# A fused attention and expert kernel: the second MLP's input weights get their tiles at the upper end of SBUF during attention, and are converted in another order

## The chip, the core and the metric

One core of a Trainium2 chip. The time is device time of one execution, in microseconds (us), of the whole program; a profiled execution gives the trace. Engines: PE multiplies, DVE and ACT do elementwise work, POOL (GpSimd) too, SP starts nearly all DMAs. Each engine works through its own list of instructions in order; they wait for one another by semaphores.

## What is computed

Attention over 4 sequences of 576 positions, 8 heads of 64, as a coarse part (every 4 positions averaged, softmax over 144) plus a local part (a band of 3 to either side); its rows x (2304 x 512) go through eight experts, one for each row, and then a second MLP:

```python
attn_out = coarse(q, k, v) repeated 4 times along the sequence + local(q, k, v)
e = argmax(x @ w_gate + bias[modality]);  x = gate * (relu(x @ w1[e]) @ w2[e])
h = x @ w_in                              # 512 -> 2048
out = (max(h,0) + alpha*min(h,0)) @ w_out # 2048 -> 512
```

`w_in` and `w_out` arrive as float64. The products behind the gate are done in three passes over a high and a low half (f32r) of each operand, so each weight is converted: 64-bit words to float32, then split into two halves.

## The kernel before

The stages follow one another. **Attention** (to about 261 us): `down(b)` is a list of steps for one sequence's coarse part (stageA transposes, stageV averages v on POOL, stageB, stageT, stageE, stageP); they are laid between the 24 local tiles of 96 rows (`local1a` to `gate3`). For each tile the gate is the product `lg` on PE, then small steps on DVE (`l`, maximum, index, one-hot `oh`), then the rank product `rk`, whose rows are scattered by POOL. The coarse part of sequence b+1 is made beside the tiles of sequence b, so it is done when sequence 3 begins (n = 18 of 24). Rows of the fullest expert start early (`Early`, products `ph` and `py`, five groups): their products stand in PE's list between those of the tiles. The last count `cnt` then leads into `plan` (some 45 small DVE steps), which fills the table `r_tab` from which SP takes where rows are loaded. At `tc.If(rare>0)` each engine loads a flag and branches; the block behind it isn't run here.

**Slots** (seven, to about 450 us): each takes 256 rows of one expert. `load_x(s+2)` asks for rows L, POOL scales them, DVE transposes (T) and splits them; PE makes `h` (96 products of 256 columns) and `y` (96); ACT and DVE make the halves `hh` and `hl` of h and those of the weights (`w1h`/`w1l`, `w2h`/`w2l`). **Second MLP** (`moe2`): five blocks of rows, `oh` then `oy`; in block 0 the 32 pieces of w_out are converted as they are needed (`W2out`).

A piece of w_in is 128 rows x 256 columns; there are 32. `W2in_load(i)` asks for one (256 KB, on SP, into a ring of three stage buffers `raw64`, shared with w_out), and `from64` converts it: L555, L556, L557 on DVE into one of two float32 tiles, the cast `wih` on ACT, the subtraction `wil` on DVE (for w_out: `wol` on POOL). The tiles wih and wil (64 KB of each partition) are opened behind attention. Pieces 0 and 1 stand behind the first slot's row preparation, 2 to 23 in the slots (four in each, from f = 0 to 3), 24 to 31 in block 0.

```python
            if f<4 and 4*s+f<22:
                with tc.issue_after(d.ins), tc.issue_after(after[0].ins): W2in(AT0+4*s+f)
```

Pools are taken from SBUF in the order of the code, and a tile laid on memory of a closed pool waits for the last reader there. The order of each engine's list is set by a scheduler from the order and priorities of the code.

Of the kernel before, what the change touches and what calls it, by code (L numbers as in the profile page):

```python
# [16 lines left out]
def attention(ctx, tc, q, k, v, mod, wg, bias, xs, running, ps, eps, zeros, early):  # L17
# [7 lines left out]
    loading=ExitStack(); ld=loading.enter_context(tc.tile_pool(name="a_load",bufs=1))  # L25
# [43 lines left out]
    KD=cp.tile([128,4,2,GD],F32,name="kdb"); nc.gpsimd.memset(KD,0.0)  # L69
    QD=cp.tile([128,4,2,GT],F32,name="qdb"); nc.gpsimd.memset(QD,0.0)  # L70
# [17 lines left out]
    KB=[cp.tile([128,4,2,SP],F32,name=f"kb{i}") for i in range(2)]  # L88
    QT=[cp.tile([128,4,SP],F32,name=f"qt{i}") for i in range(2)]
# [100 lines left out]
    def stageB(b,pair):  # L190

        e=ed[b,pair]=wk.tile([128,2,GD],F32,tag="ed",name=f"ed{b}{pair}",bufs=4)
# [3 lines left out]
        if pair==0: ek[b]=wk.tile([128,H,GT],F32,tag="ek",name=f"ek{b}",bufs=1)  # L196
# [3 lines left out]
    def stageT(b):  # L200

        e=wk.tile([128,1,GD],F32,tag="edt",name=f"edt{b}",bufs=1)
# [5 lines left out]
        eb=wk.tile([128,H,GT],F32,tag="eb",name=f"eb{b}",bufs=1)  # L208
# [3 lines left out]
    def stageE(b,i):  # L212
        if i==0: EM[b]=wk.tile([128,H,GD],F32,tag="em",name=f"em{b}",bufs=1)
# [165 lines left out]
class Router:  # L379

    def __init__(self, tc, rp, cp):
# [24 lines left out]
        self.xr=rp.tile([1,NSP],I32,name="r_xr"); self.yl=rp.tile([1,1],I32,name="r_yl"); self.ok=c([1,NSP+1],"r_ok"); nc.vector.memset(self.ok[:,0:1],1.0)  # L406
        self.rare=rp.tile([1,1],I32,name="r_rare"); self.tab0=rp.tile([1,4],I32,name="r_tab0")
# [221 lines left out]
def moe(tc, stack, router, wts, rows, ep, fp, W2in):  # L629
# [67 lines left out]
    def slot(s):  # L697
# [13 lines left out]
        for f in range(8):  # L711
# [13 lines left out]
            if f<4 and 4*s+f<22:  # L725
                with tc.issue_after(d.ins), tc.issue_after(after[0].ins): W2in(AT0+4*s+f)
# [40 lines left out]
def moe2(tc, stack, wp, tp, fp, ep, win, first, W2out, W2in, al, ysT, ytok, out):  # L767
# [12 lines left out]
    def block(j):  # L780
# [43 lines left out]
def body(tc,q,k,v,mod,wg,bias,w1,w2,w_in,w_out,alpha,out):  # L824
    nc=tc.nc
    with ExitStack() as ctx:
# [10 lines left out]
        early=Early(tc,ep,eps,rows,wts)  # L837
        with ExitStack() as a:
# [5 lines left out]
            for n in attention(a,tc,q,k,v,mod,wg,bias,xs,running,ps,eps,lambda: rows.zeros(E*N),early):  # L844
# [8 lines left out]
                if n in EARLY:  # L853
# [6 lines left out]
        wip=ctx.enter_context(tc.tile_pool(name="w_in",bufs=1))  # L860
        wir=wip.tile([128,4,F2],F32R,name="wih"); wil=wip.tile([128,4,F2],F32R,name="wil")
        fp=ctx.enter_context(tc.tile_pool(name="first",bufs=1))
        wst=ctx.enter_context(tc.tile_pool(name="w_stage",bufs=3))
        staged={}
        def w_out_rows(f,u):
            r=staged[f,u]=wst.tile([128,256,2],I32,tag="raw64",name=f"wo{f}{u}")
            nc.sync.dma_start(r.rearrange("p d w -> p (d w)"),w_out[128*f:128*f+128,256*u:256*u+256].bitcast(I32))


        PIECES=[(c,p) for c in (3,2,1,0) for p in range(6)]+[(c,p) for p in range(6,8) for c in range(4)]  # L870
        def W2in_load(i):
# [64 lines left out]
```

## Time and profile before

| | |
|---|---|
| three runs | 852.78, 853.17 and 861.1 us, median 853.17 |
| profiled execution | 859.48 us, its span 857.7 us |
| busy in the span | PE 806.6 us (94%), DVE 536.4 (63%), ACT 361.1 (42%), POOL 193.6 (23%) |
| mean granted clock of PE | 0.972 of 2.4 GHz |
| moved by DMA | 71.73 MB, 84 GB/s on average |

PE's busy time is a bad measure of how full PE is, since products are pipelined; what it loses is read from its idle stretches and from what ended them. Times in rows count from the span's start.

### The profile page before, as it was taken

To read this page: it belongs to the slowest core of one execution; us is meant where nothing else is said; L and a number is where in the kernel's file an instruction comes from. 1 tells how busy PE (TensorE), PEld (TensorE's weight loads), DVE (VectorE), ACT (ScalarE), POOL (GpSimd) and SP (SyncE) were. 2 spreads that over 40 slices of the span, in tenths; PEclk is the share of its full clock that TensorE was granted. 3 is DMA by queue.
4 is the path that set the end of the run, shared out by engine and by line. 5 is a ranking of instruction groups with operands and counts; after the bars stand their busy time and mean duration, and the time that the engine had idled before them with its cause. 6 is when DMAs were issued, how large, how long until landed. Compare 5 with 4: busy or idle time off the path is not lost.

```text
span 857.7 us, 16919 instructions
## 1 busy us (share of the span) xinstructions
PE 806.6 (94%) x6247; PEld 694.5 (81%) x6247; DVE 536.4 (63%) x1365; ACT 361.1 (42%) x863; POOL 193.6 (23%) x390
## 2 busy tenths in 40 slices
PE   4799898989998889999999998999999999999997
PEld 3477687768898889999998867888888888888895
DVE  6866857557525789999859899563344333533361
ACT  7698686786422655666542233221111111111120
POOL 9424645337441000111002223200010001000100
PEclk9779989989999999999999999999999999999999
DMA  7745666322313432459313344200020001000100
GB/s 194 174 104 156 190 186 170 98 48 55 87 45 97 88 101 75 101 118 288 78 38 103 119 138 143 88 26 1 3 83 7 1 1 62 6 1 1 49 2 24
DMA packets 96608, 71.73 MB, mean 84 GB/s; under 512 B 40456, under 2 KB 83976, under 8 KB 96520
## 3 DMA queue, kind: packets, MB, share of 16 engines
q1 hardware_dynamic: 93544, 61.02, 27.2%
q0 software_dynamic: 2976, 9.59, 3.1%
q8 instruction: 50, 0.82, 0.4%
q14 instruction: 38, 0.31, 0.2%
HBM read 76.43 MB, written 18.90 MB: 111 GB/s over the span
## 4 chain that ended last, share of the span: by engine, by line
PE 48%; DVE 9%; DMA 5%; issue 3%; ACT 1%; SPq 1%; POOL 0%; POOLq 0%; DVEq 0%; ACTq 0%
PE oh L798 18%; PE oy L787 18%; PE h L719 6%; PE y L739 6%; DMA wo<-in_moe_w_out 2%; DVE xwo L557 1%; DMA oT<-ysT 1%; DMA L<-xs 1%; DVE xwo L556 1%; DVE w1l L548 1%; DVE xwo L555 1%; DMA wi<-in_moe_w_in 1%; DVE m L800 1%; DVE m L801 1%; DVE xwi L557 1%
## 5 line engine op out<-in xcount | busy, mean ns | idle before, releaser
L547 ACT CAST gh<-m 128x512 fp32r<-128x512 f32 (+1 forms) x80 | 44.5, 557 | 230.7 <-DVE m L801 227.7
L798 PE MATMUL oh<-oxh,wih 128*128 128x512 f32 (+1 forms) x320 | 117.6, 367 | 0.0
L798 PE MATMUL oh<-oxl,wih 128*128 128x512 f32 (+1 forms) x320 | 117.6, 367 | 0.0
L798 PE MATMUL oh<-oxh,wil 128*128 128x512 f32 (+1 forms) x320 | 117.6, 367 | 0.0
L787 PE MATMUL oy<-woh,gh 128*128 128x512 f32 x272 | 106.2, 393 | 3.3 <-ACT woh L547 3.2
L787 PE MATMUL oy<-wol,gh 128*128 128x512 f32 x272 | 107.0, 394 | 1.1 <-POOL wol L548 1.1
L800 DVE TENSOR_SCALAR m<-oh,al 128x512 f32<-128x512 f32 (+1 forms) x80 | 55.5, 694 | 83.5 <-PE oh L798 83.5
L787 PE MATMUL oy<-woh,gl 128*128 128x512 f32 x272 | 106.0, 391 | 0.0
L815 POOL DMA_INDIRECT out<-o,tt x18 | 18.0, 998 | 279.9 <-ACT o L814 244.6
L548 DVE TENSOR_TENSOR gl<-m,gh 128x512 fp32r<-128x512 f32 (+1 forms) x80 | 49.2, 615 | 36.6 <-ACT gh L547 36.4
L719 PE MATMUL h<-xh,w1h 128*128 128x256 f32 x224 | 63.6, 285 | 6.9 <-DVE hl L722 6.9
L798 PEld LDWEIGHTS oh<-oxh,wil 128*128 128x128 f32 x320 | 60.2, 188 | 10.6
L798 PEld LDWEIGHTS oh<-oxh,wih 128*128 128x128 f32 x320 | 60.1, 188 | 10.6
L798 PEld LDWEIGHTS oh<-oxl,wih 128*128 128x128 f32 x320 | 60.2, 188 | 10.0
L787 PEld LDWEIGHTS oy<-woh,gh 128*128 128x128 f32 x272 | 51.3, 189 | 15.1 <-ACT woh L547 4.9
L719 PE MATMUL h<-xh,w1l 128*128 128x256 f32 x224 | 63.2, 282 | 0.1
L719 PE MATMUL h<-xl,w1h 128*128 128x256 f32 x224 | 63.1, 282 | 0.0
L787 PEld LDWEIGHTS oy<-wol,gh 128*128 128x128 f32 x272 | 51.4, 189 | 12.5 <-POOL wol L548 2.5
L739 PE MATMUL y<-hh,w2h 128*128 128x256 f32 x224 | 60.9, 280 | 0.0
L739 PE MATMUL y<-hh,w2l 128*128 128x256 f32 x224 | 60.6, 280 | 0.1
L787 PEld LDWEIGHTS oy<-woh,gl 128*128 128x128 f32 x272 | 51.5, 189 | 10.6
L739 PE MATMUL y<-hl,w2h 128*128 128x256 f32 x224 | 58.7, 280 | 0.5 <-DVE hl L722 0.5
(305 smaller groups left out, 1821.1 us busy)
## 6 DMA issues: line engine op xcount, KB each, us to landing
wraw<-in_moe_w SPq DMA_DIRECT2D x56, 512.0 KB
wi<-in_moe_w_in SPq DMA_DIRECT2D x32, 256.0 KB
wo<-in_moe_w_out SPq DMA_DIRECT2D x32, 256.0 KB
vw<-in_v SPq DMA_DIRECT2D x88, 64.0 KB
xs<-z SPq DMA_DIRECT2D x8, 528.0 KB
ldq<-in_q SPq DMA_DIRECT2D x16, 256.0 KB
ldk<-in_k SPq DMA_DIRECT2D x16, 256.0 KB
ldv<-in_v SPq DMA_DIRECT2D x8, 512.0 KB
```

The source lines that it names most:

```text
L547: nc.scalar.copy(hi,x)
L548: return lo_engine.tensor_tensor(out=lo,in0=x,in1=hi.bitcast(F32),op=ALU.subtract)
L555: nc.vector.tensor_scalar(out=xi,in0=hw,scalar1=0x07ffffff,scalar2=3,op0=ALU.bitwise_and,op1=ALU.logical_shift_left)
L556: nc.vector.scalar_tensor_tensor(out=xi,in0=lw,scalar=29,in1=xi,op0=ALU.logical_shift_right,op1=ALU.bitwise_or)
L557: nc.vector.scalar_tensor_tensor(out=xi,in0=hw,scalar=-(1<<30),in1=xi,op0=ALU.bitwise_and,op1=ALU.bitwise_or)
L719: nc.tensor.matmul(h,lhsT=a[:,c],rhs=b[:,c],start=n==0,stop=n==11); n+=1
L739: nc.tensor.matmul(y,lhsT=a[:,f],rhs=b,start=n==0,stop=n==23); n+=1
L787: nc.tensor.matmul(y[t],lhsT=a[:,ts],rhs=b[:,f],start=f==0 and k==0,stop=f==15 and k==2)
L798: nc.tensor.matmul(h[:,:n],lhsT=a[:,c,fs],rhs=b[:,c],start=k==0,stop=k==11); k+=1
L800: nc.vector.tensor_scalar(out=m[:,:n],in0=h[:,:n],scalar1=0.0,scalar2=al[:,f:f+1],op0=ALU.min,op1=ALU.mult)
L801: nc.vector.scalar_tensor_tensor(out=g[:,:n],in0=h[:,:n],scalar=0.0,in1=m[:,:n],op0=ALU.max,op1=ALU.add)
L815: nc.gpsimd.indirect_dma_start(out=out[:],out_offset=bass.IndirectOffsetOnAxis(ap=ti[:,t:t+1],axis=0),in_=o[:],in_offset=None,bounds_check ...
```

## The change

Attention's pools for tiles that only the coarse part uses (with KB and QT of the even sequences) move to the upper end of SBUF and are closed when sequence 3's tiles begin. There the tiles of w_in and the stage ring are opened at once. Two pieces are converted behind each of the last eight tiles (`TAIL`, 16 pieces), two behind the first slot's row preparation as before, two in each of the seven slots (`SLOT`, at f = 1 and 3), and none in block 0. The pieces now go by columns first (p, then c). A one-element tile shares another's memory.

```diff
-    loading=ExitStack(); ld=loading.enter_context(tc.tile_pool(name="a_load",bufs=1))
+    loading=ExitStack(); gp,gk,ld=[loading.enter_context(tc.tile_pool(name=n,bufs=1,side="right")) for n in ("a_gone","a_down","a_load")]
...
-    KD=cp.tile([128,4,2,GD],F32,name="kdb"); nc.gpsimd.memset(KD,0.0)
+    KD=gp.tile([128,4,2,GD],F32,name="kdb"); nc.gpsimd.memset(KD,0.0)
...
-            vd[b]=wk.tile([128,H,D],F32,tag="vd",name=f"vd{b}",bufs=2)
+            vd[b]=gk.tile([128,H,D],F32,tag="vd",name=f"vd{b}",bufs=2)
...
         at(local1b,n+2); go()
+        if n==len(seq)-NT:
+            assert not fill; loading.close()
         yield n
-    loading.close()
...
-LEAD=1; WLOAD=tuple([0, 0, 1, 2, 2, 3, 3, 4]); EARLY=tuple([3, 6, 10, 14, 16]); AT0=2; LATE=28
+LEAD=1; WLOAD=tuple([0, 0, 1, 2, 2, 3, 3, 4]); EARLY=tuple([3, 6, 10, 14, 16]); AT0=2; TAIL=dict.fromkeys(range(16,24),2); SLOT=(1,3); LATE=28
...
-            if f<4 and 4*s+f<22:
-                with tc.issue_after(d.ins), tc.issue_after(after[0].ins): W2in(AT0+4*s+f)
+            if f in SLOT:
+                with tc.issue_after(d.ins), tc.issue_after(after[0].ins): W2in()
...
                 W2out(f,woh,wol)
-                if f<8: W2in(f)
...
+        win=[]; staged={}; done=set()
+        def open_w_in():
+            wip=ctx.enter_context(tc.tile_pool(name="w_in",bufs=1,side="right"))
+            win.extend((wip.tile([128,4,F2],F32R,name="wih"),wip.tile([128,4,F2],F32R,name="wil")))
+            win.append(ctx.enter_context(tc.tile_pool(name="w_stage",bufs=3,side="right")))
+            W2in_load(0)
...
+        PIECES=[(c,p) for p in range(8) for c in range(4)]
...
+        def W2in(ahead=2):
+            i=len(done)
+            if i>=len(PIECES): return
+            for j in range(i+1,i+ahead+1):
+                if ("in",j) not in staged and j not in done: W2in_load(j)
+            c,p=PIECES[i]; ps=slice(256*p,256*p+256); done.add(i)
+            from64(nc,win[2],f"wi{c}{p}",win[0][:,c,ps],win[1][:,c,ps],staged.pop(("in",i)),nc.vector)
...
+                if n==min(TAIL): open_w_in()
+                for _ in range(TAIL.get(n,0)): W2in()
             with tc.high_priority(500): router.plan(psum,running,cp)
```

What this makes of the engines' lists, at three places. (The number behind a tile's name is its buffer; lines of the changed kernel are one to three higher.)

DVE, in the tail, from the rank of one tile (`jk`, `ng`) to the gate `l` of the next; before, with the gate steps ahead of it:

```order
L287 TENSOR_TENSOR xts_4109<-pv_4100,ot_3532 128x384
L306 TENSOR_TENSOR oh_3946<-io_294,i_3943 96x8
L313 RECIPROCAL x_126<-ng_3948 96x4
L326 ISA jk_4035,ng_3948<-rk_4029,oh_3946 96x8
L326 ISA ng_3948 96x1
L581 STREAM_TRANSPOSE Te_3498<-Le_3492 128x512
L301 TENSOR_TENSOR l_4065<-lg_4052,bsel 96x8
```

The same place now:

```order
L326 ISA jk_4087,ng_3984<-rk_4081,oh_3982 96x8
L326 ISA ng_3984 96x1
L549 TENSOR_TENSOR wil<-xwi_4338,wih 128x256
L558 SCALAR_TENSOR_TENSOR xwi_4346<-wi_4264,xwi_4346 128x256
L556 TENSOR_SCALAR xwi_4412<-wi_4336 128x256
L549 TENSOR_TENSOR wil<-xwi_4346,wih 128x256
L557 SCALAR_TENSOR_TENSOR xwi_4412<-wi_4336,xwi_4412 128x256
L556 TENSOR_SCALAR xwi_4420<-wi_4344 128x256
L558 SCALAR_TENSOR_TENSOR xwi_4412<-wi_4336,xwi_4412 128x256
L557 SCALAR_TENSOR_TENSOR xwi_4420<-wi_4344,xwi_4420 128x256
L301 TENSOR_TENSOR l_4117<-lg_4104,bsel 96x8
```

Eight steps of conversions stand where one transposition stood.

PE, from the last count to the branch, before:

```order
L410 MATMUL cnt<-running_4361,r_one 1x8
L932 BRANCH_PREFETCH_HINT
L602 MATMUL py_3803<-eh_3501,wraw 128x128 x8
L602 MATMUL ph_3860<-Te_3835,wraw 128x128 x4
L602 MATMUL ph_3866<-Te_3835,wraw 128x128 x4
L602 MATMUL ph_3872<-Te_3835,wraw 128x128 x4
L602 MATMUL ph_3902<-Te_3835,wraw 128x128 x4
L602 MATMUL ph_3964<-Te_3835,wraw 128x128 x4
L602 MATMUL ph_3987<-Te_3835,wraw 128x128 x4
L602 MATMUL ph_3993<-Te_3835,wraw 128x128 x4
L602 MATMUL ph_3999<-Te_3835,wraw 128x128 x4
L602 MATMUL py_4080<-eh_3838,wraw 128x128 x8
```

Behind these comes the branch (L901). Now:

```order
L411 MATMUL cnt<-running_4493,r_one 1x8
L935 BRANCH_PREFETCH_HINT
L603 MATMUL ph_4039<-Te_3843,wraw 128x128 x4
L603 MATMUL ph_4045<-Te_3843,wraw 128x128 x4
L603 MATMUL ph_4051<-Te_3843,wraw 128x128 x4
L603 MATMUL py_4132<-eh_3846,wraw 128x128 x8
L524 TENSOR_LOAD r_rare
L903 COMPARE_AND_BRANCH
```

Of 48 early products behind the count 20 are left; 28 moved ahead of it.

SP, from the last weight load of slot 0 to the rows L of slot 2, before:

```order
L542 DMA wraw<-in_moe_w 128x8x128
L520 TENSOR_LOAD r_tab x2
L567 ISA
L567 DMA xs<-z 1024x1x132
L875 DMA wi_10263<-in_moe_w_in 128x512
L875 DMA wi_10546<-in_moe_w_in 128x512
L520 TENSOR_LOAD r_tab
L572 ISA
L572 DMA L_10340<-xs 32x8x132
```

And now:

```order
L543 DMA wraw<-in_moe_w 128x8x128
L521 TENSOR_LOAD r_tab x2
L568 ISA
L568 DMA xs<-z 1024x1x132
L852 DMA wi_10687<-in_moe_w_in 128x512
L521 TENSOR_LOAD r_tab
L573 ISA
L573 DMA L_10459<-xs 32x8x132
```

One load of w_in stands ahead of the rows where two stood.

## Rows read from the trace of the kernel before

**Rows 1.** Busy time by stretch: us, busy (x instructions), granted clock, DMA share, GB/s

```profile
core 0: us, PE busy (x) PEld busy (x) DVE busy (x) ACT busy (x) POOL busy (x), PEclk, DMA share, GB/s
200.00:220.00 20.00, 20.00 (x367) 16.71 (x362) 14.63 (x76) 12.15 (x44) 15.19 (x36) 1.00 0.28 65
220.00:240.00 20.00, 20.00 (x229) 17.52 (x228) 8.02 (x42) 7.77 (x24) 8.02 (x18) 1.00 0.29 72
...
360.00:380.00 20.00, 19.32 (x163) 18.92 (x162) 19.29 (x44) 11.92 (x26) 0.00 (x0) 1.00 0.43 124
380.00:400.00 20.00, 18.18 (x156) 17.78 (x155) 19.16 (x38) 13.17 (x29) 2.42 (x1) 1.00 0.91 225
460.00:480.00 20.00, 20.00 (x90) 16.57 (x89) 18.21 (x41) 5.70 (x12) 3.45 (x5) 1.00 0.33 104
...
520.00:540.00 20.00, 17.83 (x71) 14.06 (x70) 19.76 (x41) 6.21 (x14) 7.66 (x11) 0.91 0.38 120
```

**Rows 2.** PE's waits, whole span: us in total, times, longest us

```profile
PE h L719 <- DVE hl L722: 6.9, 6, 3.0
...
PE py L602 <- SPq L901: 3.3, 1, 3.3
PE oy L787 <- ACT woh L547: 3.2, 3, 1.7
```

**Rows 3.** Costliest groups, PE: busy, mean ns, idle before and releaser

```profile
L787 PE MATMUL oy<-wol,gh 128*128 128x512 f32 x272 | 107.0, 394 | 1.1 <-POOL wol L548 1.1
...
L739 PE MATMUL y<-hl,w2h 128*128 128x256 f32 x224 | 58.7, 280 | 0.5 <-DVE hl L722 0.5
```

**Rows 4.** Timeline of PE: start us, us, what, [idle before it and releaser]

```profile
283.16 2.05 PE L602 MATMUL py<-eh,wraw 128*128 128x128 f32 x16 [1.71 <-ACT eo L611]
...
318.15 0.53 PE L719 MATMUL h<-xh,w1h 128*128 128x256 f32 x1 [3.00 <-DVE hl L722]
...
532.54 0.50 PE L787 MATMUL oy<-woh,gh 128*128 128x512 f32 x1 [1.73 <-ACT woh L547]
```

**Rows 5.** Busy time by stretch, behind three waits of PE (columns as in Rows 1)

```profile
318.00:322.00 4.00, 3.85 (x19) 3.86 (x20) 4.00 (x9) 2.26 (x6) 0.00 (x0) 0.57 0.28 91
532.00:537.00 5.00, 4.01 (x10) 2.98 (x11) 4.89 (x10) 1.21 (x3) 2.34 (x3) 0.66 0.50 159
275.00:279.00 4.00, 3.69 (x33) 3.69 (x34) 2.13 (x6) 0.93 (x2) 0.00 (x0) 1.00 0.02 6
```

**Rows 6.** Timeline of PE from the last count to behind the branch

```profile
260.94 0.17 PE L410 MATMUL cnt<-running,r_one 96*1 96x8 bf16 x1
...
262.93 7.31 PE L602 MATMUL ph<-Te,wraw 128*128 128x128 f32 x64
270.07 1.95 PE L602 MATMUL py<-eh,wraw 128*128 128x128 f32 x16
275.31 0.94 PE L602 MATMUL py<-eh,wraw 128*128 128x128 f32 x6 [3.29 <-SPq L901]
```

**Rows 7.** Timeline of DVE in a slot, a stretch without idle

```profile
309.98 0.28 DVE L555 TENSOR_SCALAR xwi<-wi 128x256 int32<-128x256 int32 x1
310.18 0.42 DVE L722 SCALAR_TENSOR_TENSOR hl<-h,hh 128x256 fp32r<-128x256 f32 x1
...
311.31 0.42 DVE L556 SCALAR_TENSOR_TENSOR xwi<-wi,xwi 128x256 int32<-128x256 int32 x1
311.65 0.42 DVE L741 COPY yo<-y 128x256 f32<-128x256 f32 x1
```

**Rows 8.** Timeline of SP's queue, then of DVE, ahead of 318.15

```profile
300.39 4.83 SPq L875 DMA_DIRECT2D wi<-in_moe_w_in  x2
305.80 1.93 SPq L572 DMA_DIRECT2D L<-xs  x4
...
315.94 1.25 DVE L581 STREAM_TRANSPOSE T<-L 128x1024 f32<-128x1024 f32 x1 [3.21 <-POOL L L579]
```

**Rows 9.** Conversions of w_out on DVE: duration ns min/median/max, first and last start

```profile
L556 DVE SCALAR_TENSOR_TENSOR xwo<-wo,xwo x32: 408/416/966, 421.4 to 538.5; 128x256 int32<-128x256 int32 x32
L557 DVE SCALAR_TENSOR_TENSOR xwo<-wo,xwo x32: 409/420/968, 423.3 to 540.0; 128x256 int32<-128x256 int32 x32
```

More of the change, by code (lines that the diff above doesn't have):

```diff
@@ L87, in attention @@
     BD=[cp.tile([128,H,TT],F32,name=f"bd{i}") for i in range(3)]
-    KB=[cp.tile([128,4,2,SP],F32,name=f"kb{i}") for i in range(2)]
-    QT=[cp.tile([128,4,SP],F32,name=f"qt{i}") for i in range(2)]
+    KB=[p.tile([128,4,2,SP],F32,name=f"kb{i}") for i,p in enumerate((gp,cp))]
+    QT=[p.tile([128,4,SP],F32,name=f"qt{i}") for i,p in enumerate((gp,cp))]
     VW=[cp.tile([128,H,D],F32,name=f"vw{i}") for i in range(3)]
@@ L131, in stageA @@
     def stageA(b,pair,n):
-        if pair==0 and n=="q": qd[b]=wk.tile([128,4,128],F32,tag="qd",name=f"qd{b}",bufs=1)
+        if pair==0 and n=="q": qd[b]=gk.tile([128,4,128],F32,tag="qd",name=f"qd{b}",bufs=1)
         L=loads.pop((b,n,pair)); T=(QT if n=="q" else KB)[b%2]
@@ L168, in stageV0 @@
             L=L.rearrange("p h (r d) -> p r h d",r=4); o=vd[b][:,4*part:4*part+4]
-            o1=wk.tile([128,4,D],F32,tag="vs",name=f"vs{b}{part}",bufs=1)
+            o1=gk.tile([128,4,D],F32,tag="vs",name=f"vs{b}{part}",bufs=1)
             nc.gpsimd.tensor_tensor(out=o,in0=L[:,0],in1=L[:,1],op=ALU.add)
@@ L200, in stageT @@
     def stageT(b):
-        e=wk.tile([128,1,GD],F32,tag="edt",name=f"edt{b}",bufs=1)
+        e=gk.tile([128,1,GD],F32,tag="edt",name=f"edt{b}",bufs=1)
         p=psum([128,1,GD],f"sd{b}t")
@@ L212, in stageE @@
     def stageE(b,i):
-        if i==0: EM[b]=wk.tile([128,H,GD],F32,tag="em",name=f"em{b}",bufs=1)
+        if i==0: EM[b]=gk.tile([128,H,GD],F32,tag="em",name=f"em{b}",bufs=1)
         if i<2:
@@ L765, in rows2, with moe2 @@
     return load,(hi,lo,ti)
-def moe2(tc, stack, wp, tp, fp, ep, win, first, W2out, W2in, al, ysT, ytok, out):
+def moe2(tc, stack, wp, tp, fp, ep, win, first, W2out, al, ysT, ytok, out):
     nc=tc.nc
@@ L837, in body, with w_out_rows, W2in_load, W2out @@
         early=Early(tc,ep,eps,rows,wts)
+        win=[]; staged={}; done=set()
[4 more added lines that the diff above has]
+            W2in_load(0)
+        def w_out_rows(f,u):
+            r=staged[f,u]=win[2].tile([128,256,2],I32,tag="raw64",name=f"wo{f}{u}")
+            nc.sync.dma_start(r.rearrange("p d w -> p (d w)"),w_out[128*f:128*f+128,256*u:256*u+256].bitcast(I32))
+        PIECES=[(c,p) for p in range(8) for c in range(4)]
+        def W2in_load(i):
+            if i>=len(PIECES): return
+            c,p=PIECES[i]
+            r=staged["in",i]=win[2].tile([128,256,2],I32,tag="raw64",name=f"wi{c}{p}")
+            router.marks[ENG.SP]=nc.sync.dma_start(r.rearrange("p d w -> p (d w)"),w_in[128*c:128*c+128,256*p:256*p+256].bitcast(I32))
+        def W2in(ahead=2):
+            i=len(done)
+            if i>=len(PIECES): return
+            for j in range(i+1,i+ahead+1):
+                if ("in",j) not in staged and j not in done: W2in_load(j)
+            c,p=PIECES[i]; ps=slice(256*p,256*p+256); done.add(i)
+            from64(nc,win[2],f"wi{c}{p}",win[0][:,c,ps],win[1][:,c,ps],staged.pop(("in",i)),nc.vector)
+        def W2out(f,woh,wol):
+            for u in range(2):
+                if (f,u) not in staged: w_out_rows(f,u)
+                c=slice(256*u,256*u+256)
+                from64(nc,win[2],f"wo{f}{u}",woh[:,f,c],wol[:,f,c],staged.pop((f,u)),nc.gpsimd)
         with ExitStack() as a:
@@ L899, in body @@
             with tc.issue_after(a[0].ins), tc.issue_after(a[1].ins):
-                for i in range(AT0): W2in(i)
+                for i in range(AT0): W2in()
             with tc.If(rare>0,label="rare"): every()
@@ L908, in body @@
         with ExitStack() as s2:
-            moe2(tc,s2,wp,rp,fp,ep,(wir,wil),first,W2out,lambda f: W2in(24+f,1),al,ysT,ytok,out)
+            moe2(tc,s2,wp,rp,fp,ep,win[:2],first,W2out,al,ysT,ytok,out)
 _INS = ["q", "k", "v", "moe_modality_id", "moe_w_gate", "moe_modality_bias", "moe_w1", "moe_w2", "moe2_w_in", "moe2_w_out", "moe2_alpha"]
```

42 lines of the change are left out of this document (9 added, 33 removed).

## Prediction

> **What bounds the kernel now.** I read the busy table by stretches first [rows 1]. From 200 to 240 us (the last tiles of attention) PE is busy without a gap while DVE has 14.63 and 8.02 of 20 us to do: there PE sets the pace. From 360 to 400 (the expert slots) DVE is at 19.29 and 19.16 of 20 and PE falls to 19.32 and 18.18; from 520 to 540 (second MLP, block 0) DVE is at 19.76 and PE at 17.83. In these two stages DVE is full and PE waits for it. The list of PE's waits then gives sizes [rows 2, 3]: 6.9 us of `h` and 0.5 of `y` on the low halves `hl` (slots), 3.2 and 1.1 on the halves of w_out (block 0), and one wait of 3.3 for SP at the branch between attention and slots. The timeline shows the two largest of the first kinds, 3.00 at 318.15 and 1.73 at 532.54 [rows 4]; behind both the granted clock fell, to means of 0.57 over 4 us and 0.66 over 5 us [rows 5], so part of these stretches ran at the lower level, 1.2 GHz. Half clock costs (1-0.57) x 4 = 1.7 us and (1-0.66) x 5 = 1.7 us more. Behind the 3.29 us at the branch it stayed at 1.00 [rows 5, 6]. All that DVE costs PE behind the branch is thus 7.4+1.7 = 9.1 us in the slots and 4.3+1.7 = 6.0 us in block 0. From about 541 us on PE runs alone, and nothing of the change is there.
>
> **The change, part by part.**
>
> *Price of a conversion.* Three DVE steps (L555 to L557), an ACT cast and a DVE subtraction. Where DVE is never idle the next instruction starts 0.20 us behind L555 and 0.33 to 0.34 behind L556 [rows 7]; L557 and L548 of that tile are like L556. One piece is 0.20 + 3 x 0.34 = 1.2 us of DVE. Thirty-two pieces remain, in other places: before 2 at the slots' head, 22 in slots, 8 in block 0; now 16 in the tail, 2 at the head, 14 in slots, none in block 0.
>
> *Block 0: -6.0 us.* Eight pieces, 9.8 us of DVE, leave a stage where DVE has 18.21 and 19.76 of 20. The w_out ring (three buffers) is no longer shared, and in the order five w_out loads are issued before the last store of the slots, where three were. DVE gets 9.8 us free of some 80; the waits to cover are 4.3. I take all: 6.0. Bounds: 0 (if the w_out loads were the limit) and 6.0.
>
> *Slots: -6.9 us.* Eight pieces fewer, again 9.8 us of DVE. The 3.00 us wait is a queue matter: SP holds two w_in loads from 300.39 for 4.83 us since no stage buffer is free, the rows of a later slot are asked for at 305.80 only, and DVE sits 3.21 us at 315.94 before it can transpose them, with `hl` behind [rows 8]. In the new SP order one w_in load, with a buffer freed in slot 0, stands ahead of those rows, where two did. I take the whole 3.0+1.7, and half of the other 4.4, as DVE will still be some 85 to 90% full: 6.9. Bounds 0 and 9.1.
>
> *Later count: +6.4 us.* This speaks against the change. The scheduler, with 16 pieces on DVE in the tail, lets each gate come later and fills PE with early expert rows meanwhile. In PE's order 48 early products stood behind `cnt` and in front of the branch; now 20 do. 32 of them take 7.31 us [rows 6] (the trace writes each as two), 0.228 each, so 28 more ahead of `cnt` put it 28 x 0.228 = 6.4 us later. What follows `cnt` is a chain that PE has no part in (plan on DVE, table and row loads on SP, the branch): PE resumes 275.31-260.94 = 14.4 us behind it. Before, 11.1 us of that was covered, and 3.29 were idle; now 20 x 0.228 = 4.6 is covered and about 9.8 idle. Early products before the branch are the same 184 from stageT on, so nothing is won for it. I take 6.4; only a shorter chain would make it less, and its steps are all there in the new order: both bounds 6.4.
>
> *Tail: +3 us.* Up to the gate of the fourth tile from the end, behind which the last conversion stands, DVE had 14.63+8.02 = 22.7 us in 40; with 16 x 1.22 = 19.5 it has 42.2. PE's order puts 24 more early products ahead of that gate (92 for 68), so the time there is 40+5.5 = 45.5 us: 93% full. In the slots at 96% PE lost 0.7 and 1.8 us in 20 [rows 1]. Two such stretches are 1.4 to 3.6. I take 3. Bounds: 0 (PE never idled in the tail and DVE often waited for PE there) and 10 (below). ACT's 16 casts go into its free time. The 16 loads, 4.2 MB over 40 us, add 105 GB/s to 65 and 72 where the DMA share is 0.28 and 0.29. They stand on SP ahead of later `vw` and `Le` loads, each held until a buffer is free; `vw` is loaded three tiles ahead, which hides it. The first `wil` waits until the coarse part is read out; the order puts it behind the first `xts` that uses it. Both are costed at nothing but belong to the bound of 10.
>
> *Clock behind the longer wait: +0.5 us.* 9.8 us idle is over three times what stood before a fall at 318.15, so I expect one, worth 1.7 us [rows 5]. But at 283.16 PE waits 1.71 us for ACT, held up by casts [rows 4]; if PE arrives late that wait shrinks. Bounds 0 and 3.4 (two such falls).
>
> Sum: -6.0 -6.9 +6.4 +3.0 +0.5 = **-3.0 us**. The profiled run took 859.5 us, so 856.5 by its own measure; it is 6.3 above the median of the runs, 853.2, to which I apply the same difference: **850.2 us**. Where the 6.3 us lie I can't see; if they lie in the waits that go, the gain is smaller.
>
> **A page against a row.** Conversions of w_out in block 0 have medians of 0.416 and 0.420 us and maxima of 0.966 and 0.968 [rows 9]; in that stage POOL runs the subtraction `wol` beside them. In the tail POOL is busy 15.19+8.02 = 23.2 of 40 us [rows 1], mostly with tile work.
> The Trainium skill (SBUF — State Buffer, section "SBUF: two separate sides") says that a DVE instruction with two SBUF inputs and a GpSimd instruction that reads SBUF shut each other out for a whole instruction. By that rule the tail would be dearer than the medians make it, as in the first rival, and the sum +4.0 instead of -3.0; the maxima agree with it, the medians show that most instructions escape.
>
> **Rivals.**
> - *DVE becomes the bound of the tail.* 48 of the moved instructions read two SBUF tiles; at POOL's 58% share, and 0.55 us more for each that is hit (0.97 less 0.42), DVE has 48 x 0.58 x 0.55 = 15 us more; 3.3 were free, and about 2 can be made up behind the last conversion: +10 instead of +3. The page named above has this as its rule. Sum +4.0, 857.2; with less of the slots' gain up to 860. For: those maxima. Against: POOL's tile work thins out after 220 (8.02 of 20). It decides from a tail of 6 us on; beyond that the change is slower than before. Chance 0.18.
> - *The slots keep their waits.* DVE's order still has the transposition and low halves ahead of `hl`, so only block 0's gain and 2.4 us come: -6.0 -2.4 +6.4 +3.0 +0.5 = +1.5, 854.7. For: four of the six waits are under 1 us and may come from order alone. Against: the largest has a cause that goes. Chance 0.17.
> - *All waits go and the tail is free:* -6.0 -9.1 -1.7 (ACT at 283.16) +6.4 = -10.4, 842.8. For: no idle of PE in the tail before. Against: 93% on an in-order engine. Chance 0.15.
> - The forecast, 846 to 855: 0.50.
>
> **How the numbers follow.** About 1% (8.5 us) is what a measurement of this kernel can tell from no change, as its own three runs span 852.8 to 861.1. The range 843 to 859 leaves out the upper part of the first rival and half of the third, some 0.18. Faster by over 1% (under 844.6) is most of the third: 0.15. Slower by over 1% (over 861.7) is the first with lost gains: 0.10. Within 1%: 0.75.
>
> **What would show it.** In the new profile: `cnt` some 6 to 10 us later and PE's wait for SP near 10 us where 3.29 stood; a lower clock just behind it; `oy` waiting under 1 us in all; `h` on `hl` 2 to 3 us in all, none of 3.00; DVE above 18 of 20 us from 215 to 240. I am wrong if `cnt` stays near 261, if PE idles over 6 us in the tail, or if block 0 still waits for w_out.

## The result, and the profile after

The changed kernel takes 861.3 us (median of 20 runs, 856.6 to 867.9) where the kernel before, measured beside it, takes 856.4 (20 runs, 851.9 to 861.5): a ratio of 1.0068, with a 95% interval of 1.0044 to 1.0091, so it is slower by some 5.8 us. I had forecast 850.2 against 853.2, that is 3.0 us less, and a range up to 859. The sign is wrong and the time is outside the range. (Measured beside it, the kernel before, too, is 3.2 us above the 853.2 from which the range was built; the sign doesn't hang on that.)

Below, "the tail" is the stretch from the last coarse product `sd3t` to the last `cnt`, in numbers from the last of the 16 `sd3t` products to `cnt` (the grouped rows show the first of the 16, 0.4 us earlier); "the branch" is from there to the first `h` of the slots; "behind" is from that `h` to the last `oy`. The part ahead of the tail differs by several us between executions whatever the kernel (the tail began between 198 and 205 us in all traces), so I compare stretches, not whole spans, and leave the verdicts on time to the ratios.

| stretch, us | before | after | forecast of the difference |
|---|---|---|---|
| tail | 59.4 | 79.5 | +9.4 (later count 6.4, tail 3.0) |
| branch | 18.0 | 20.1 | +0.5 |
| behind | 572.1 | 554.1 | -12.9 (slots 6.9, block 0 6.0) |

The timeline of PE of the changed kernel (start us, us, what, idle before and releaser), first the tail and then the branch; of [rows 6] `cnt` stood at 260.94 and the wait for SP was 3.29:

```profile
198.38 0.72 PE L206 MATMUL sd3t<-kdb,qdb 128*32 128x144 f32 x16
...
216.84 0.88 PE L284 MATMUL pv<-bd,vw 128*64 128x96 f32 x16 [1.95 <-DVE xts L287]
...
247.46 0.28 PE L295 MATMUL xb<-ident,xts 128*96 128x128 f32 x1 [3.39 <-DVE xts L287]
...
278.29 0.17 PE L411 MATMUL cnt<-running,r_one 96*1 96x8 bf16 x1
...
293.01 5.66 PE L603 MATMUL py<-eh,wraw 128*128 128x128 f32 x32 [9.90 <-SPq L903]
```

Two waits for `xts` stand in the tail, where PE had never waited before. From 195 to 560 us these, the branch and one wait of 1.2 are all that the list of PE's waits holds (us in total, times, longest):

```profile
PE py L603 <- SPq L903: 9.9, 1, 9.9
PE xb L295 <- DVE xts L287: 3.4, 1, 3.4
PE pv L284 <- DVE xts L287: 2.0, 1, 2.0
PE py L603 <- ACT eo L612: 1.2, 1, 1.2
```

Of [rows 2, 3] the waits of `h`, `y` and `oy` for halves are gone, 11.7 us in all. Busy time by stretch (columns as in [rows 1]), first of the stages, then behind the three longer waits:

```profile
200.00:220.00 20.00, 18.05 (x321) 15.01 (x323) 14.79 (x68) 10.00 (x34) 12.40 (x26) 0.96 0.45 125
220.00:240.00 20.00, 20.00 (x200) 17.15 (x193) 17.09 (x71) 10.30 (x31) 7.99 (x16) 0.96 0.60 131
240.00:260.00 20.00, 16.61 (x138) 14.85 (x138) 9.96 (x40) 4.90 (x18) 4.55 (x11) 0.74 0.49 124
...
380.00:400.00 20.00, 20.00 (x172) 20.00 (x171) 18.12 (x32) 12.97 (x27) 2.38 (x1) 1.00 0.70 170
520.00:540.00 20.00, 20.00 (x90) 16.57 (x89) 16.23 (x31) 5.97 (x12) 5.10 (x6) 1.00 0.24 74
```

```profile
218.00:222.00 4.00, 4.00 (x64) 3.43 (x58) 3.94 (x13) 2.34 (x6) 1.39 (x2) 0.57 0.51 120
249.00:259.00 10.00, 10.00 (x70) 9.17 (x69) 5.74 (x24) 2.70 (x9) 2.68 (x8) 0.50 0.51 151
286.00:297.00 11.00, 3.99 (x19) 3.99 (x20) 3.84 (x8) 1.79 (x3) 1.91 (x1) 0.53 0.22 50
```

In the slots and block 0 PE is busy throughout. In the tail the granted clock falls to 1.2 GHz behind both waits: 4 us at a mean of 0.57 (1.7 us lost) and 10 us at 0.50 (5.0 lost). The tail's 20.1 us more are thus 5.3 of idle time, 6.7 of half clock, 6.4 of the 28 early products that now stand ahead of `cnt`, and 1.7 that I can't place. That is a list of what PE did, not yet of causes.

DVE is not full while PE waits (17.09, then 9.96 of 20). Its timeline ahead of 247.46, and SP's queue before that:

```profile
239.02 0.41 DVE L558 SCALAR_TENSOR_TENSOR xwi<-wi,xwi 128x256 int32<-128x256 int32 x1
243.43 0.30 DVE L556 TENSOR_SCALAR xwi<-wi 128x256 int32<-128x256 int32 x1 [4.00 <-DMA wi<-in_moe_w_in]
...
245.81 0.30 DVE L556 TENSOR_SCALAR xwi<-wi 128x256 int32<-128x256 int32 x1 [1.42 <-DMA wi<-in_moe_w_in]
...
246.77 0.55 DVE L287 TENSOR_TENSOR xts<-pv,ot 128x384 f32<-128x384 f32 x1
```

```profile
233.68 1.99 SPq L573 DMA_DIRECT2D Le<-xs  x4
236.35 0.33 SPq L585 DMA_DIRECT2D ytok<-Le  x1
236.77 3.02 SPq L852 DMA_DIRECT2D wi<-in_moe_w_in  x3
```

The product `pv` that `xts` adds up had ended by 236.2. `xts` started 10.6 us later, since two pieces stood ahead of it in DVE's list, and DVE waited 4.00 and 1.42 us for their loads. The first of these was asked for at 236.77 only, behind the rows `Le` of an early slice and that slice's small store `ytok`, and was in use 6.7 us later; piece 0, asked for at 197.81, was being converted at 200.9. By the trace's marks of landing, the three loads of w_in asked for from 236.77 to 239.46 took 6.6 to 8.5 us and the other fifteen from 197 to 255 us took 2.7 to 4.2. What slows these three isn't shown.

The first wait, 1.95 us at 216.84, has no load of w_in in it. POOL, then DVE, ahead of it:

```profile
214.64 1.05 POOL L580 TENSOR_TENSOR Le<-Le 128x512 f32<-128x512 f32 x1 [2.24 <-DMA ytok<-Le]
...
215.93 0.21 POOL L312 TENSOR_SCALAR ng<-ng 96x1 f32<-96x1 f32 x1
```

```profile
216.17 0.18 DVE L313 RECIPROCAL x<-ng 96x4 f32<-96x4 f32 x1 [2.24 <-POOL ng L312]
216.27 0.52 DVE L287 TENSOR_TENSOR xts<-pv,ot 128x384 f32<-128x384 f32 x1
```

POOL stands 2.24 us for a transfer of an early slice; the gate's `ng` is behind that in POOL's list, and on DVE `xts` is behind the step that needs `ng`. This first `xts` starts 17.5 us behind the last `sd3t` (216.27 less 198.81); in the kernel before it was 14.0 (215.56 less 201.56).

### The profile page after: what moved, and what is told of

It reads as the page before. It is cut to its first block, busy times and chain, and to the rows that moved or that the text cites. A ratio compares the mean times of both kernels' runs of the same rounds, so it can differ in the third digit from the quotient of the medians.

```text
span 859.3 us, 16912 instructions
## 1 busy us (share of the span) xinstructions
PE 805.9 (94%) x6247; PEld 697.0 (81%) x6247; DVE 536.4 (62%) x1365; ACT 361.0 (42%) x863; POOL 197.9 (23%) x390
## 4 chain that ended last, share of the span: by engine, by line
PE 63%; ACT 1%; issue 1%; DMA 0%; POOLq 0%; ACTq 0%
PE oh L798 23%; PE oy L788 22%; PE y L740 9%; PE h L720 9%; DMA out<-o,tt 0%; ACT w2h L548 0%; PE py L603 0%; POOLq L935 0%; ACT w1h L548 0%; ACT wih L548 0%; ACT o L814 0%; ACT eo L612 0%; ACTq L548 0%; POOLq L815 0%
## 5 line engine op out<-in xcount | busy, mean ns | idle before, releaser
L548 ACT CAST gh<-m 128x512 fp32r<-128x512 f32 (+1 forms) x80 | 44.6, 557 | 243.6 <-DVE m L801 236.2
L798 PEld LDWEIGHTS oh<-oxh,wih 128*128 128x128 f32 x320 | 60.1, 188 | 10.6
```

What stands on the lines that cost most here:

```text
L548: nc.scalar.copy(hi,x)
L798: nc.tensor.matmul(h[:,:n],lhsT=a[:,c,fs],rhs=b[:,c],start=k==0,stop=k==11); k+=1
```

## The experiments

Each ratio is to the kernel before, run beside it, with its 95% interval; one hundredth is 8.6 us, and intervals of differences between two kernels are put together from both. The edits are against the changed kernel unless another is named; a line is shown by its part that changes, and `...` stands for lines between. The table has every trace's stretches; of cover40 only the time is used.

| kernel | ratio (interval) | tail | branch | behind |
|---|---|---|---|---|
| changed kernel | 1.0068 (1.0044-1.0091) | 79.5 | 20.1 | 554.1 |
| place_only | 1.0037 (1.0011-1.0062) | 59.4 | 19.3 | 567.6 |
| no_tail_conv | 0.9825 (0.9779-0.9870) | 59.1 | 23.1 | 551.3 |
| one_load | 0.9941 (0.9910-0.9973) | 70.9 | 19.0 | 555.4 |
| ring5 | 1.0024 (0.9991-1.0058) | 72.2 | 18.9 | 552.9 |
| cover40 | 1.0046 (1.0010-1.0081) | | | |
| ring5_cover40 | 1.0054 (1.0029-1.0080) | 75.1 | 22.3 | 550.8 |
| one_load_cover40 | 0.9951 (0.9925-0.9978) | 73.0 | 21.4 | 551.5 |
| half8 | 1.0014 (0.9985-1.0043) | 68.9 | 20.9 | 556.1 |
| late8 | 0.9986 (0.9955-1.0016) | 64.0 | 21.4 | 557.9 |
| spread16 | 0.9964 (0.9940-0.9989) | 73.1 | 20.9 | 552.6 |
| half8_pool | 0.9945 (0.9919-0.9972) | 66.7 | 21.2 | 553.8 |
| ring5_pool | 0.9961 (0.9934-0.9988) | 69.6 | 21.1 | 551.7 |
| place_pool | 1.0102 (1.0070-1.0134) | 59.4 | 19.7 | 575.0 |
| half8_pool_late4 | 0.9972 (0.9945-0.9999) | 68.7 | 18.7 | 554.5 |
| late8_pool | 0.9950 (0.9925-0.9975) | 67.0 | 20.8 | 555.1 |
| spread8_pool | 0.9940 (0.9916-0.9964) | 64.1 | 20.0 | 559.1 |
| spread16_pool | 0.9960 (0.9931-0.9989) | 68.3 | 21.0 | 553.7 |
| spread16_ring5_pool | 0.9928 (0.9898-0.9958) | 69.0 | 21.0 | 548.7 |

**The place of the tiles alone: place_only.**

```diff
-TAIL=dict.fromkeys(range(16,24),2)
+TAIL=dict.fromkeys(range(16,24),0)
-            if f in SLOT:
+            if f<4 and 4*s+f<22:
...
                 W2out(f,woh,wol)
+                if f<8: W2in()
```

> The tiles of w_in are opened at the upper end of SBUF at the same tile of attention as in the changed kernel, but the tail converts nothing: 22 conversions stand in the slots and 8 in block 0, as before the change. PE's order ahead of the count is that of the kernel before (48 early products behind `cnt`). If only the tail's conversions cost time (all three theories below), the time is that of the kernel before, 856.4 +- 2 us, the stretch from the last coarse score (`sd3t`) to `cnt` is 60 +- 1.5 us, and the wait at the branch 3 to 4. If the place of the tiles or their early opening costs something by itself (port, release of buffers), the time is over 859.

The tail is that of the kernel before, 59.4. So the tail's 20 us come from the conversions there, not from the opened tiles. The time is 1.0037 of before, 3.2 us more (0.9 to 5.3), while its trace has the branch 1.3 us longer and the stretch behind it 4.5 shorter; where the loss lies I can't say. By the mark set beforehand (over 859 where the kernel before takes 856.4, that is 2.6 us more) the place or the early opening costs something by itself, though the interval reaches below that mark. no_tail_conv has both too, so its gain below is net of this.

**The gain alone: no_tail_conv.**

```diff
-            W2in_load(0)
+            done.update(range(16)); W2in_load(16)
-TAIL=dict.fromkeys(range(16,24),2)
+TAIL=dict.fromkeys(range(16,24),0)
...
                 for i in range(AT0): W2in()
+                for w in win[:2]: nc.gpsimd.memset(w[:,:,:1024].bitcast(F32),0.5)
```

> The tail's 16 conversions and their loads are left out; the first half of w_in's columns hold a constant written by GpSimd at the slots' head. Slots and block 0 are those of the changed kernel, the tail is that of the kernel before. This shows what the change can give behind the branch when the tail costs nothing. By the forecast, 12.9 us below the kernel before; by the changed kernel's trace (from the first product of the slots to the last of the second MLP 554.1 us against 572.1) 18 us below, some 836 to 838 by the measure in which the kernel before takes 854.5. If the gain shown there was a matter of one execution, less than 10.

GpSimd wrote the constants at 217 us, in the tail, and not at the slots' head; the tail is 59.1 all the same. The ratio, from four runs, is 15.0 us of gain (11.1 to 18.9). The 12.9 that I had summed for slots and block 0 lie in it. In its trace this is a stretch behind that is 20.8 us shorter than before and a branch that is 5.1 longer. The tail's conversions cost the rest: 1.0068 less 0.9825 is 20.8 us, where the forecast had 9.9 for tail, count and clock.

**Late loads or DVE's work: one_load and ring5.**

```diff
             c,p=PIECES[i]
+            if 3<=i<16: staged["in",i]=kept[i%3]; return
             r=staged["in",i]=win[2].tile(
+            if i<3: kept.append(r)
```

> The tail's 16 conversions read three stage buffers that are loaded once; the loads of pieces 3 to 15 are left out, so those columns of w_in hold wrong numbers. DVE's work is the same. Theory A (late loads: a piece's steps wait in DVE's in-order queue for its 256 KB load, and `xts` behind them): DVE's waits for wi (5.9 us in the changed kernel) go, PE's waits for `xts` (5.3) and the half-clock stretches behind them go, and the stretch `sd3t` to `cnt` falls from 79.9 to 67 to 70; time 10 us below the changed kernel, some 851. Theory B (DVE's 19.5 us of conversion work itself is what the tail can't hold): the stretch stays within 2 us of 79.9 and the time within 2 us of the changed kernel. Theory C (28 early products moved ahead of `cnt`): the part of 6.4 us stays in both cases.

```diff
+            win.append(ring.enter_context(tc.tile_pool(name="w_tail",bufs=5,side="right")))
...
-            r=staged["in",i]=win[2].tile(
+            r=staged["in",i]=win[3 if i<16 else 2].tile(
-        def W2in(ahead=2):
+        def W2in(ahead=4):
-            for j in range(i+1,i+ahead+1):
+            for j in range(i+1,min(i+ahead+1,16) if i<14 else i+3):
```

> The tail's pieces get five stage buffers instead of three and are asked for up to four pieces ahead instead of two. Theory A with the ring as the cause of the late loads: DVE's waits for wi fall below 1.5 us, the stretch `sd3t` to `cnt` to 69 to 74 us, time 6 to 10 us below the changed kernel. Theory A with SP's order as the cause (the load stands behind the rows of an early slice): one wait of 2 to 4 us stays, time 0 to 3 us below. Theory B: no change within 2 us.

With the same work on DVE and (but for 0.6 us) no loads to wait for, the kernel is 0.0127 lower, 10.9 us (7.5 to 14.2); the tail falls from 79.5 to 70.9, PE's waits there are

```profile
PE pv L284 <- DVE xts L287: 2.0, 2, 1.8
```

and the half clock in the tail is gone. Theory A holds for half of the 20.8. Five buffers instead of three give 3.8 us (0.3 to 7.3): DVE still waits 3.8 us for loads, once 3.2. That one is for a load asked for at 239.90, again straight behind a slice's `ytok`; it took 8.7 us to land (those ahead of it 2.6 to 5.0), so more buffers alone don't end the waits. The other half, 0.9941 against 0.9825 or 9.9 us (5.2 to 14.5), stays with hardly a load late.

**The products moved ahead of the count: cover40, ring5_cover40, one_load_cover40.** The same edit to the changed kernel, to ring5 and to one_load:

```diff
+BEHIND=54
...
-        if k==NSP-1: self.held=LATE
+        if k==NSP-1: self.held=LATE+BEHIND
...
-        early.go(len(early.steps))
+        early.held=LATE
+        with tc.issue_after(router.marks[ENG.PE].ins): early.go(len(early.steps))
```

> As the changed kernel, but the fifth early slice's products before the branch are all put behind `cnt`: 40 early products cover the branch instead of 20 (48 in the kernel before). Theory C (their place costs 0.228 us each): `cnt` comes 4.6 us earlier, the wait at the branch falls from 9.9 to about 5.3, and the time falls by 4.6, by 6 if the half clock behind the branch goes too. Theories A and B (the tail waits for DVE): with less to fill, PE idles in the tail instead, `cnt` moves by less than 1.5 us, and the time stays within 1.5 us of the changed kernel.

> Five stage buffers in the tail and 40 early products behind `cnt` instead of 16. Theory C: the tail, no longer held by loads, is bound by PE's order, so `cnt` comes 24 x 0.228 = 5.5 us earlier than with five buffers alone (72.2 from `sd3t` to 66.7), the wait at the branch falls from 10.0 to 4 or 5, its half clock of 10.2 us (5.1 us lost) goes: 5 to 10 us below ring5, some 848 by the measure in which the kernel before takes 854.5. Theories A and B: the tail waits for DVE either way; PE idles there instead, time within 2 us of ring5.

> No loads for pieces 3 to 15 (those columns of w_in hold wrong numbers) and 40 early products behind `cnt` instead of 16. With no load to wait for, only DVE's work is left in the tail. Theory C: `sd3t` to `cnt` falls from 70.9 to 65.4, the branch wait from 8.9 to 3.4, time 5 to 8 us below one_load. Theory B: DVE's work holds `cnt` at 70 to 71, PE idles 4 to 5 us more for `xts` or the gate, time within 2 us of one_load.

The differences to their pairs are -0.0022, +0.0030 and +0.0010, each uncertain by some 0.0042; theory C expected -0.005 to -0.012. The first pair alone doesn't rule that out (4.6 us were expected there); the other two do. In one_load_cover40 the wait at the branch is indeed 2.6 instead of 8.9, but `cnt` comes no earlier: the tail is 73.0 instead of 70.9. Without the filler PE waits for DVE and GpSimd, and behind the first of these waits the clock falls, 8 us at a mean of 0.57 that one_load ran at 1.00:

```profile
PE rk L319 <- DVE oh L306: 1.9, 2, 1.0
PE xb L295 <- DVE xts L287: 1.8, 1, 1.8
...
PE cnt L411 <- POOL running L324: 0.4, 1, 0.4
```

```profile
223.00:231.00 8.00, 8.00 (x89) 6.67 (x89) 5.79 (x25) 3.09 (x10) 2.52 (x7) 0.57 0.24 60
```

So the 28 moved products are not a cost of their own. They fill time in which the gate waits for DVE; taken away, that time is idle or runs at the lower clock.

**How many pieces: half8.**

```diff
-AT0=2; TAIL=dict.fromkeys(range(16,24),2); SLOT=(1,3)
+AT0=3; TAIL=dict.fromkeys(range(16,24),1); SLOT=(1,2,3)
```

> Eight conversions in the tail, one for each of the last eight tiles, three at the slots' head and 21 in the slots; block 0 has none. Theory A (late loads on a ring of three): a piece every 8 us leaves each load two tiles of time, so PE's waits for `xts` in the tail go and no half clock stands there; `sd3t` to `cnt` is 59.4 + 24 early products of 0.228 = 65 us, against 79.5 in the changed kernel and 59.4 before; block 0's waits for w_out (4.3 us before) are gone, the slots' (7.4 before) are back, as DVE is as full there as before. Time 6 to 9 us below the changed kernel, that is 2 to 4 us below or level with the kernel before. Theory B (work alone): half of the excess stays, 8 us, and the time is some 2 us below the changed kernel.

4.6 us below the changed kernel (1.4 to 7.8) and level with before. The tail is 68.9, half of the excess: theory B's size, though the half clock in the tail did go, as theory A had it. One piece for each tile in the code is not one for each tile in the list: the scheduler put all eight ahead of the fifth `xts`, as early as they were ready.

**Where they stand on DVE: late8 and spread16.**

```diff
-        nc.vector.tensor_tensor(out=xt.rearrange(
+        early.sum=nc.vector.tensor_tensor(out=xt.rearrange(
...
-                for _ in range(TAIL.get(n,0)): W2in()
+                if n in TAIL:
+                    with tc.issue_after(early.sum.ins):
+                        for _ in range(TAIL[n]): W2in()
```

spread16 is that alone; late8 adds to half8 that and `TAIL={16:0,**dict.fromkeys(range(19,23),2)}`.

> The changed kernel, its 16 pieces queued on DVE two behind each `xts` of the last sequence and six behind the last one, instead of up to four ahead of the next `xts`. Same work, same loads, three stage buffers. Theory P: `sd3t` to `cnt` falls from 79.5 to 72 to 76, the waits for `xts` (5.3) go, but six pieces behind the last `xts` (7.3 us) stand ahead of the plan's first step on DVE and may hold it; time 3 to 6 us below the changed kernel, ratio 1.000 to 1.003. Theory W: within 2 us of the changed kernel, ratio 1.005 to 1.009.

> As half8 (8 pieces in the tail, 3 at the slots' head, 21 in the slots), but two pieces each are queued on DVE behind the sums `xts` of the last three tiles, and two more behind the last: in half8 all eight stand ahead of the fifth `xts` of the last sequence. Theory P (the place in DVE's order costs, since DVE is fuller early in the tail and its queue is in order): `sd3t` to `cnt` falls from 68.9 to 61 to 64, no wait of PE for `xts`, time 5 to 7 us below half8, ratio to the kernel before 0.993 to 0.996. Theory W (the amount of DVE's work costs wherever it stands in the tail): `sd3t` to `cnt` 67 to 70 and the time within 2 us of half8.

The same 16 pieces and the same loads on three buffers, queued behind `xts` instead of ahead, are 8.9 us cheaper (6.0 to 11.8), more than I expected, and faster than before. DVE still waits 3.2 us for loads, but PE waits 0.8 us for `xts` where it waited 5.3:

```profile
PE py L603 <- SPq L905: 11.1, 1, 11.1
PE ph L603 <- ACT eh L608: 0.9, 1, 0.9
PE xb L295 <- DVE xts L287: 0.8, 1, 0.8
```

A late load thus costs when the piece that needs it stands ahead of something that PE waits for. Not all of the gain is that: here, and in late8, no piece stands ahead of the first `xts` either, which starts 13.7 us behind `sd3t`, where it was 17.5 in the changed kernel and still 17.3 in one_load and half8. The 13 loads that one_load leaves out (3.4 MB) could also cost by their traffic alone; spread16 keeps them all and gains 8.9, which speaks against that. With eight pieces the later place shortens the tail in the trace from 68.9 to 64.0, as theory P had it, but 2.4 us in the time are within the uncertainty (3.6): in that execution the waits of `h` for `hl` in the slots were 4.7 us, where half8 had 3.0.

**The last step on GpSimd: half8_pool, ring5_pool, place_pool.**

```diff
-staged.pop(("in",i)),nc.vector)
+staged.pop(("in",i)),nc.gpsimd)
```

> As half8, but the last step of every w_in conversion (`wil`, the subtraction) runs on GpSimd, which has 2 of 20 us to do in the slots, instead of on DVE: 0.34 of 1.22 us of DVE for each of the 32 pieces less. Theory B (DVE's work is what a piece costs wherever DVE is full or near it): in the tail 8 x 0.34 = 2.7 us less of DVE, `sd3t` to `cnt` 66 to 67 instead of 68.9; in the slots 21 x 0.34 = 7 us less, the waits of PE there (4.9 in half8) under 2; time 4 to 6 us below half8, ratio to the kernel before 0.994 to 0.997. Rival (GpSimd and DVE hinder each other at SBUF, or GpSimd's own queue delays `running` and the gate in the tail): no gain or a loss against half8.

> As ring5 (16 pieces in the tail on five stage buffers), with `wil` on GpSimd. Theory B: 16 x 0.34 = 5.4 us of DVE less in the tail, `sd3t` to `cnt` 67 to 69 instead of 72.2, slots no longer waiting for DVE; time 4 to 6 us below ring5, ratio to the kernel before 0.995 to 0.998. Rival (GpSimd, 8 to 12 of 20 us busy there, becomes late with the gate's steps): `sd3t` to `cnt` stays at 72 or grows.

> As place_only (no conversion in the tail, 22 in the slots, 8 in block 0), with `wil` on GpSimd. If DVE's fullness in the slots and block 0 is what costs there, 30 x 0.34 = 10 us of DVE less take most of PE's waits for `hl` (8.2 us) and part of those for w_out (4.4 us), as no_tail_conv's gain of 15 us came from 16 pieces, 20 us of DVE: time 5 to 8 us below place_only, ratio to the kernel before 0.994 to 0.998, with the tail as before (59.4). Rival (hindering at SBUF): DVE's steps get longer in the slots (L557 above 0.45 us in the median) and the gain is under 2 us.

half8 gains 5.9 us (2.5 to 9.3), ring5 5.4 (1.7 to 9.1); both are now faster than before. GpSimd takes longer for the step than DVE's 0.416, but has the time:

```profile
L549 POOL TENSOR_TENSOR wil<-xwi,wih x32: 724/742/2165, 220.5 to 441.1; 128x256 fp32r<-128x256 f32 x32
```

Where nothing is converted in the tail, the same edit loses 5.6 us (2.1 to 9.1), against my expectation. Eight of its pieces are in block 0, where GpSimd already makes the low halves of w_out; there PE's wait for w_out's high half is 5.5 us instead of place_only's 3.3:

```profile
PE oy L788 <- ACT woh L548: 5.5, 4, 2.8
```

Behind two of its waits, at 381 and 535 us, the granted clock falls too (means of 0.66 over 5 us and 0.57 over 8, some 5 us lost), where place_only has one such fall (0.57 over 4 us, 1.7 lost). The rest of that loss isn't explained.

**Filling the branch: half8_pool_late4** (half8_pool with `LATE=4`).

> As half8_pool, but 4 steps of the last early slice instead of 28 are kept for behind the branch: 58 early products stand between `cnt` and the branch (36 in half8_pool), 13.2 us of the chain's 14.4. If the idle time at the branch is a cost that products from behind it can fill, PE's wait there falls from 7.1 to 1 to 2 us, the half clock of 6.8 us behind it (3.4 us lost) goes, the first product of the slots comes 18 to 19 us behind `cnt` instead of 21.2, and the time is 2 to 5 us below half8_pool, ratio to the kernel before 0.989 to 0.992. Rival: the first product waits for its weights (`w1h`, `w1l`), converted only behind the branch, some 19 us behind `cnt` anyway; then PE idles behind the branch instead of ahead of it, and the time is within 2 us of half8_pool.

The wait for SP is gone and the first `h` comes 2.4 us earlier behind `cnt`, but the time is not lower (+2.3 us, uncertain by 3.2). PE now waits for the first weight half, converted only behind the branch:

```profile
292.46 0.58 PE L720 MATMUL h<-xh,w1h 128*128 128x256 f32 x1 [4.59 <-ACT w1h L548]
```

**Do the removals add up: late8_pool, spread8_pool, spread16_pool, spread16_ring5_pool.** Combinations of the edits above.

> late8 with the last step of each conversion on GpSimd. Theory P: `sd3t` to `cnt` 61 to 64 (half8_pool 66.7), slots as in half8_pool; time 3 to 5 us below half8_pool, ratio to the kernel before 0.988 to 0.991. Theory W: as half8_pool, 0.993 to 0.997.

> half8_pool with one piece queued behind each `xts` of the last sequence and two more behind the last. Theory P: between half8_pool and late8_pool, `sd3t` to `cnt` 63 to 66, ratio to the kernel before 0.990 to 0.994. Theory W: as half8_pool, 0.993 to 0.997.

> The changed kernel with its 16 tail pieces queued on DVE behind the sums `xts` (as spread16) and the last step of every piece on GpSimd. If place and work are separate costs, `sd3t` to `cnt` falls from 73.1 (spread16) to 68 to 70 and the time by 3 to 5 us more: ratio to the kernel before 0.990 to 0.993. If they are the same cost seen twice, the ratio stays at 0.995 to 0.997, as in spread16 and ring5_pool.

> As spread16_pool, with five stage buffers in the tail. If loads are still late there (3.2 us of DVE's waits for wi in spread16) and cost by themselves, `sd3t` to `cnt` is 1 to 3 us shorter than in spread16_pool and the time 1 to 3 us less. If a piece behind `xts` that waits for its load no longer holds PE, both are equal within 1.5 us.

They don't: all four lie between 0.9928 and 0.9960 with overlapping intervals, which half8_pool (0.9945) and ring5_pool (0.9961) overlap as well. Place alone gained 8.9 us and GpSimd alone 5.4 to 5.9 (on ring5 and half8), but spread16_pool with both is 9.2 below the changed kernel (6.1 to 12.4). So place, late loads and DVE's work are largely one cost. That it is the time by which the gate's steps on DVE are late fits the traces, but no run shows it by itself. By the ratio, the lowest, spread16_ring5_pool, is 6.2 us below the kernel before (3.6 to 8.7) and some 12 below the changed kernel. It is still 8.8 us (4.1 to 13.5) above no_tail_conv: that much of the tail's cost none of these edits takes away.

## Why the prediction was wrong

- **The step that failed is "Tail: +3 us".** Together with "Later count" it held 9.4 us; the trace has 20.1. I had priced DVE's work and concluded 93% full. DVE was less full than that, 17.09 and 9.96 of 20, and PE waited all the same. The loads I had "costed at nothing": each "held until a buffer is free" on SP, hidden because `vw` is loaded ahead. I asked whether they delay other transfers and not what stands behind a piece that waits for its load: DVE's list is in order, and `xts` was behind it. Late loads are worth half of the tail's 20.8 us (one_load), and queueing the pieces behind `xts` gains 8.9 with loads still late (spread16). The other item "costed at nothing" came as well: the first `wil`, behind the coarse part. ACT's first cast of w_in stands straight behind the last `ot` copy, at 213.79, and between 202.3 and 218.2 no piece was begun, so 14 of the 16 fell into the 36 us behind. No run shows what this crowding costs.
- **"Later count: +6.4 us" was wrong as a mechanism.** The count of products was right and `cnt` moved; that this costs 6.4 by itself was not. In three pairs the products went back behind `cnt` and nothing was won, in two of them clearly. I had added a cause and its symptom. The 9.9 us that stay when hardly a load is late are the cost of the conversions' work, 19.5 us on DVE and 6.5 on ACT (16 casts of 0.405); how they divide between the two engines, the gate's steps and the filler isn't settled.
- **Clock: +0.5 us.** Expected behind the branch only, where it came (0.53 in 11 us, most of them idle). The branch is 2.1 us longer. The expensive falls are the two in the tail, 6.7 us, behind waits I had not expected at all.
- **Block 0 and slots, -12.9 us, held:** 15.0 (11.1 to 18.9) without the tail's work, and 18.0 in the changed kernel's trace. No wait of `oy`, none of `h` for `hl`; I had expected 2 to 3 us of the latter. The trace's 18.0 is more than both upper bounds together (15.1); place_only, where nothing goes from these stages, is shorter there by 4.5 in its trace, so some of it is the spread of single executions.
- **The wait at the branch** was forecast at 9.8 and is 9.90, the chain from `cnt` to PE's return 14.4 and 14.7.
- **The rivals.** The first (DVE becomes the bound of the tail, +10) named the place and, at 857.2, came nearest, but by luck: its mechanism didn't act. Its price was that of two-input steps shut out by GpSimd. In the tail they took

```profile
L557 DVE SCALAR_TENSOR_TENSOR xwi<-wi,xwi x16: 380/416/1153, 201.7 to 256.5; 128x256 int32<-128x256 int32 x16
L558 DVE SCALAR_TENSOR_TENSOR xwi<-wi,xwi x16: 389/414/425, 202.5 to 257.3; 128x256 int32<-128x256 int32 x16
L549 DVE TENSOR_TENSOR wil<-xwi,wih x16: 368/416/559, 216.8 to 260.2; 128x256 fp32r<-128x256 f32 x16
```

  (duration ns min/median/max), as in [rows 9]; 48 steps that lose 15 us would show medians far above 0.416. The rule of the Trainium skill (SBUF — State Buffer, section "SBUF: two separate sides") thus doesn't explain this loss; single maxima may be its doing: the step of 1.153 started at 237.48, while POOL's L580 ran from 237.29 to 238.35. The second rival fell, since the slots lost all their waits; the third had the gains of slots and block 0 right (all waits gone; of ACT's 1.7 at 283.16, a wait of 1.2 is left) and the tail, which it took for free, wrong.
- **"What would show it"** was right on the wait at the branch, the clock behind it, `oy` and the largest wait for `hl`. `cnt` came 17.3 us later, not 6 to 10, and DVE did not go above 18 of 20. I had named over 6 us of PE's idle time in the tail as what would prove me wrong: 5.3 came, and 6.7 of half clock behind it, which that test left out.

## What to carry to other kernels

Work that is moved into an engine's idle time brings its inputs' waits into that engine's list: ask, for every moved instruction that waits on a load, what stands behind it and who waits for that, before asking whether the engine has room. Queue such work behind the step that the critical engine needs, not ahead of it, and don't trust the place in the code to do so. Where a scheduler moves filler ahead of a milestone, find out what the milestone waits for before counting the filler as a cost.

## What the runs showed of the hardware that was not expected

A wait of PE can cost more behind it than itself: 3.39 us idle at 247.46 were followed by 10 us at 1.2 GHz though PE was busy for 10.00 of the 10 us, and 1.95 us at 216.84 by a shorter fall, while in one_load a wait of 1.76 us at the same place was followed by none, nor was the 3.29 us of [rows 6]. A load of 256 KB took 2.7 to 4.2 us to land in the changed kernel's tail, but 6.6 to 8.5 straight behind an early slice's rows and its store `ytok`, and there 7.5 to 8.9 in ring5 (2.6 to 5.0 elsewhere in its tail). The same subtraction of 128 x 256 elements has a median of 0.742 us on GpSimd and 0.416 on DVE.
